# All MLP steps, weight decoding included, put into one planned list of steps

## The chip, the cores and the metric

The kernel runs on one core of one Trainium2 chip. The metric is device time in microseconds (us) of one execution. TensorE is called PE, VectorE DVE, ScalarE ACT, GpSimd POOL, and SyncE, which issues all DMAs here, SP.

## The reference

Inputs are q, k, v of shape 4 x 8 x 576 x 64 and the weights of two further layers. Cut to what matters:

```
attn = softmax(mask(q k^T / 8)) v          # 8 heads, window 32, plain or with dilation 4
x    = attn as (4, 576, 512)
moe  = sum over the best 2 of 4 experts of gate * (causal attention of x with wq, wk, wv) wo[e]
xn   = (moe - mean) / sqrt(var + 1e-6) * g_ln
out  = moe + max(xn @ w_ch1, 0) @ w_ch2    # w_ch1: 512 x 2048, w_ch2: 2048 x 512, both arrive as float64
```

The change touches the last line only: the MLP and its weights. The float64 weights are read as pairs of 32-bit words and are turned into float32 pairs (high part and rest) by the kernel itself.

## The kernel before

The 2304 tokens are 18 tiles of 128 tokens. The moe result of a tile lies in `x2(i)`; it is written by a product called `pwo` (L840) and a copy. For the MLP the tiles form five groups: four of four tiles, 512 tokens each, and the last of two tiles, 256 tokens. The hidden size 2048 is cut in 16 slices f of 128. For each slice there are two weight tiles, x = 0 (from w_ch1) and x = 1 (from w_ch2).

Steps of the MLP:

- `norm_tile` (L992): a tile is centred into `xg` (one buffer, by ACT or DVE), turned by four PE transposes (`pxt`, L1008) and written as `xn`, in two halves, each by ACT (L1017) for the high part and DVE (L1019) for the rest.
- `decode(f, x)` (L884): a DMA of 512 KB into `ws` (two buffers), then a chain of one buffer each: ACT square `d_sq` (L916), DVE L920 and L922 into `d_t`, DVE L926 and L929 into `d_pw`, POOL sum L932, DVE L935, for x = 0 a POOL product with g_ln (L940), ACT cast to the high part of `wp` (L942), POOL rest (L944).
- `mlp_group(fs, gi, ...)` (L1025): for each slice in fs, 12 matmuls of 512 columns into a PSUM bank `phid` (L1043), then ACT relu into `ht` (L1051) and DVE rest (L1053). `ht` has three buffers. Then for each tile of the group, 3 matmuls per slice into a bank `pout` (L1068), and a DVE sum into x2 (L1075). At the last slice pair x2 goes out by DMA.

A job is one call of `mlp_group`. `phid` and `pout` use the three banks of tag "a" in the first jobs, and the two banks "s" and three banks "t" in the later ones.

What sets the order: inside `tc.manual_schedule()` every step is a generator that asks for engine time (`op`), buffers (`acq`) or facts (`key`). `run_chains` (L198) goes through them like a clock: each time it emits the step that can start first by its table of costs, ties by rank. What is emitted so stays in that order on each engine, and each engine runs its queue in order. Before, the list held the attention layers, norms, the decoding of slices 0 to 2, and the jobs (0, 1) and (2) for groups 0 to 2. Everything behind it (slice pair (0, 1) for groups 3 and 4, slice 3, and all later pairs) was written out by the loop at the end (`run`, `jobs`, `weights`): one weight decoding ahead of each job. These steps are outside the manual schedule, and the order on the engines shows that a scheduler of the framework then interleaves them, so they do not stand exactly as written.

Of the kernel before, what the change touches and what calls it, by code (L numbers as in the profile page):

```python
# [8 lines left out]
F32R = mybir.dt.float32r  # L9
# [14 lines left out]
def windowed_attention_moe_mlp(  # L24
# [795 lines left out]
    def out_proj(b, i):  # L820
# [21 lines left out]
        if i == 0:  # L842
            give("yhs", tp)
        elif last(("yh", b), NT - 1):
            give("yh", tp)
        t, e = yield either(("ACT", act(DM)), ("DVE", dve(DM)), deps=[tp])
# [18 lines left out]
    places.update(ht=[], ws=[], dsq=[], dt1=[], dpw=[], xg=[])  # L865

    def open_mlp():
# [10 lines left out]
        for tag, n in (("ht", 1), ("ws", 2), ("dsq", 1), ("dt1", 1), ("dpw", 1), ("xg", 1)):  # L878
            give(tag, t, n)
        put("wts", at=t)  # L880
# [3 lines left out]
    def decode(f, x):  # L884
# [20 lines left out]
        else:  # L905
            if f // GF % 2 == 0:
                w = wts.tile([P, 2, DM], F32R, tag=f"wp{f % GF}{x}", name="wp")
            else:
                w = att.tile([P, 2, DM], F32R, tag=("yh", "yl", "woh", "wol")[2 * (f % GF) + x], name="wp")
# [115 lines left out]
    def mlp_group(fs, gi, htag, otag):  # L1025
# [7 lines left out]
        hs = []  # L1033
        for f in fs:
            t0 = max(t, (yield key("wf", f, 0)))
            w1h, w1l = WF[f, 0]
            tb = yield acq(htag)
# [8 lines left out]
            ta = yield acq("ht")  # L1046
            pool, tag = HT.pop(0)
            ht = pool.tile([P, 2, 4 * P], F32R, tag=tag, name="ht")
            hh, hl = ht[:, 0], ht[:, 1]
# [7 lines left out]
        for x, i in enumerate(grp):  # L1057
# [12 lines left out]
            if x == len(grp) - 1:  # L1070
                for *_, pool, tag in hs:
                    HT.append((pool, tag))
                give("ht", tp, len(hs))
            tx = yield op("DVE", 660.0, [tp, tr])
            nc.vector.scalar_tensor_tensor(x2(i), po, rstd[:, i:i + 1], x2(i), op0=ALU.mult, op1=ALU.add)  # L1075
            give(otag, tx)
            if fs[-1] == NF - 1:
                for bb, s0, p0, m in rows_of(order[i]):
                    nc.sync.dma_start(out[bb, s0:s0 + m, :], x2(i)[p0:p0 + m])
# [5 lines left out]
    with tc.manual_schedule():  # L1085
# [21 lines left out]
        for f in range(3):  # L1107
            for x in range(2):
                chain(41.0 + 2 * f + x, decode(f, x))
# [6 lines left out]
        for gi in range(EARLY):  # L1116
            chain(44.0 + gi, mlp_group((0, 1), gi, "a", "a"))
            chain(48.0 + gi, mlp_group((2,), gi, "a", "a"))
        run_chains()


    def run(gen):
        ask = next(gen)
        while True:
            value = 0.0
            if ask[0] == "op" and len(ask[1]) > 1:
                value = 0.0, ask[1][0][0]
            try:
                ask = gen.send(value)
            except StopIteration:  # L1130
                return


    jobs = [((0, 1), gi) for gi in range(EARLY, len(groups))]
    jobs += [((3,), gi) for gi in range(EARLY)] + [((2, 3), gi) for gi in range(EARLY, len(groups))]
    for f0 in range(2 * GF, NF, GF):
        jobs += [((f0, f0 + 1), gi) for gi in range(len(groups))]

    def weights(fs):
        for f in fs:  # L1140
            for x in range(2):
                run(decode(f, x))
                yield

    fill = weights((3,))
    for x, (fs, gi) in enumerate(jobs):
        if (fs[-1], 0) not in WF:
            for _ in fill:
                pass
        if x == 0 or fs != jobs[x - 1][0]:  # L1150
            if fs != (2, 3):
                for _ in fill:
                    pass
                nf = fs[-1] + 1 if fs[-1] > 1 else 3
                fill = weights(range(nf, min(nf + GF, NF)) if nf > 3 else (3,))
        next(fill, None)
        run(mlp_group(fs, gi, "s", "t"))
# [28 lines left out]
```

## Time and profile before

| | us |
|---|---|
| median of 3 runs | 777.85 (777.27 to 781.38) |
| the profiled execution | 777.57 |
| its span on the core | 775.8 |
| PE busy | 728.6 (94%) |
| DVE busy | 535.2 (69%) |
| ACT busy | 303.4 (39%) |
| POOL busy | 207.0 (27%) |

The span begins at the first instruction of the core and ends with the last. A time such as "at 417.57" is us from the span's start. A row of a timeline gives start, length, engine, line, operation, result and operands, shapes, count, and in brackets idle time just before, with the engine and line that ended it. Neighbouring matmuls overlap in the rows: how fast they follow is read from the starts.

### The profile page before, as it was taken

Reading aid. Unit: us, or ns where it says so; the run is one execution under the profiler, and the core shown is the slowest. Engines: PE = TensorE matmul, PEld = TensorE weight load, DVE = VectorE, ACT = ScalarE, POOL = GpSimd, SP = SyncE. Lnnn points to the kernel's source line nnn. Section 1 sums busy time; section 2 is a strip of 40 time slices with the busy share of each in tenths; the row PEclk is TensorE's granted clock in tenths of the full one; section 3 lists DMA queues with packets and bytes.
Section 4 is the critical chain, followed back from the end, with each engine's and each line's share of the span. In section 5 each row is a group of like instructions: output and inputs, shape, how many; then the busy total and the mean of one; then the engine's idle time right before and its main releaser. Section 6 shows DMA issues by size and latency. Waiting matters only on the chain.

```text
span 775.8 us, 13793 instructions
## 1 busy us (share of the span) xinstructions
PE 728.6 (94%) x5196; PEld 606.8 (78%) x5196; DVE 535.2 (69%) x1357; ACT 303.4 (39%) x817; POOL 207.0 (27%) x245
## 2 busy tenths in 40 slices
PE   6788899998999998998997999999999999999997
PEld 5677778986888686876775888888888888888886
DVE  5647898599867989898657788657466475644333
ACT  4454576466555776574325222212121121211110
POOL 3242154022302234434004445214032140220000
PEclk9869999999999999899998999999999999999999
DMA  8681143033302111011001212102011010000114
GB/s 146 123 159 31 28 102 71 21 67 74 63 17 52 39 61 55 28 52 31 1 1 55 82 54 82 55 27 82 1 55 54 26 57 27 28 1 0 41 69 136
DMA packets 87890, 41.80 MB, mean 54 GB/s; under 512 B 74384, under 2 KB 83088, under 8 KB 87824
## 3 DMA queue, kind: packets, MB, share of 16 engines
q1 hardware_dynamic: 87824, 40.92, 20.9%
q8 instruction: 41, 0.67, 0.4%
q14 instruction: 25, 0.20, 0.1%
HBM read 36.19 MB, written 4.72 MB: 53 GB/s over the span
## 4 chain that ended last, share of the span: by engine, by line
PE 71%; DVE 20%; ACT 5%; DMA 2%; issue 2%; POOL 1%; DVEq 0%; SPq 0%; ACTq 0%; POOLq 0%
PE pout L1068 26%; PE phid L1043 25%; PE pp L624 3%; PE pv L521 2%; PE pwo L840 2%; PE ppt L767 2%; PE s L436 2%; DVE nm L711 1%; PE ptr L380 1%; PE ppt L464 1%; DMA nat<-in_k_dram 1%; DVE xl L497 1%; DVE klz L647 1%; DVE sc L448 1%; DVE mx L446 1%
## 5 line engine op out<-in xcount | busy, mean ns | idle before, releaser
L1043 PE MATMUL phid<-xn,wp 128*128 128x512 f32 (+1 forms) x960 | 218.0, 374 | 2.3 <-ACT xn L1017 1.2
L1068 PE MATMUL pout<-wp,ht 128*128 128x512 f32 x864 | 216.0, 395 | 0.3 <-DVE ht L1053 0.3
L1043 PEld LDWEIGHTS phid<-xn,wp 128*128 128x128 f32 x960 | 169.7, 190 | 37.0 <-ACT xn L1017 1.6
L1068 PEld LDWEIGHTS pout<-wp,ht 128*128 128x128 f32 x864 | 159.8, 188 | 36.3 <-DVE ht L1053 0.7
L1075 DVE SCALAR_TENSOR_TENSOR x2a<-pout,rstd,x2a 128x512 f32<-128x512 f32 x124 | 88.7, 746 | 90.4 <-PE pout L1068 90.3
L1051 ACT ACTIVATE ht<-phid 128x512 fp32r<-128x512 f32 (+1 forms) x80 | 44.4, 555 | 216.5 <-PE pout L1068 138.7
L944 POOL TENSOR_TENSOR wp<-d_pw,wp 128x512 fp32r<-128x512 f32 x34 | 46.1, 1357 | 149.2 <-ACT wp L942 138.3
L1053 DVE SCALAR_TENSOR_TENSOR ht<-phid,ht 128x512 fp32r<-128x512 f32 (+1 forms) x80 | 50.1, 632 | 34.2 <-ACT ht L1051 34.2
L932 POOL TENSOR_TENSOR d_pw<-d_pw,d_t 128x512 f32<-128x512 f32 x34 | 43.9, 1290 | 78.6 <-DVE d_pw L929 70.2
L745 POOL TENSOR_SCALAR Pp<-Pp,rs 128x512 f32<-128x512 f32 (+3 forms) x38 | 45.6, 1207 | 71.0 <-DVE rs L738 37.6
L457 POOL TENSOR_TENSOR sc<-sc,rs 128x288 f32<-128x288 f32 x38 | 25.2, 668 | 86.1 <-DVE rs L455 71.7
L242 ACT COPY pT<-ppt 96x384 f32<-96x384 f32 (+4 forms) x77 | 35.2, 466 | 11.0 <-PE ppt L767 8.8
L380 PE MATMUL ptr<-ident,nat 72*128 72x72 f32 (+1 forms) x196 | 26.4, 260 | 12.9 <-DMA nat<-in_q_dram 9.6
L713 ACT ACTIVATE Pp<-s,nm 128x192 f32<-128x192 f32 (+3 forms) x64 | 30.3, 474 | 18.8 <-DVE nm L711 15.0
L942 ACT CAST wp<-d_pw 128x512 fp32r<-128x512 f32 x34 | 21.1, 620 | 40.4 <-DVE d_pw L935 33.7
L696 PE MATMUL s<-KH,SQ 128*128 128x64 f32 (+4 forms) x96 | 34.1, 362 | 1.1 <-ACT Pp L713 1.1
L436 PE MATMUL s<-kT,qT 64*64 64x96 f32 x576 | 34.4, 259 | 0.2 <-ACT kT L242 0.2
L916 ACT ACTIVATE d_sq<-ws 128x512 f32<-128x512 f32 x34 | 22.8, 672 | 28.4 <-DVE d_pw L935 22.0
L380 PEld LDWEIGHTS ptr<-ident,nat 72*128 72x128 f32 (+1 forms) x196 | 20.6, 155 | 15.4 <-DMA nat<-in_q_dram 5.2
L922 DVE SCALAR_TENSOR_TENSOR d_t<-ws,d_t 128x512 int32<-128x512 int32 x34 | 32.1, 944 | 0.6
L436 PEld LDWEIGHTS s<-kT,qT 64*64 64x64 f32 x576 | 31.7, 146 | 0.5 <-issue 0.5
L464 PE MATMUL ppt<-ident,sc 128*96 128x128 f32 x144 | 26.2, 297 | 6.0 <-DVE xl L497 3.5
(164 smaller groups left out, 1374.7 us busy)
## 6 DMA issues: line engine op xcount, KB each, us to landing
ws<-in_moe_w_ch_dram SPq DMA_DIRECT2D x34, 512.0 KB, 3.4
nat<-in_q_dram SPq DMA_DIRECT2D x14, 288.0 KB, 3.7
nat<-in_k_dram SPq DMA_DIRECT2D x14, 288.0 KB
vt<-in_v_dram SPq DMA_DIRECT2D x16, 192.0 KB, 3.7
out_dram<-x2a SPq DMA_DIRECT2D x12, 256.0 KB, 2.1
vt<-in_v_dram SPq DMA_DIRECT2D x32, 48.0 KB, 1.9
out_dram<-x2b SPq DMA_DIRECT2D x4, 256.0 KB, 2.5
vt<-in_v_dram SPq DMA_DIRECT2D x16, 40.0 KB, 2.1
```

The costliest lines, as they stand in the source:

```text
L242: (nc.scalar.copy if engine == "ACT" else nc.vector.tensor_copy)(dst, src)
L380: nc.tensor.transpose(pt[:, pw * c:pw * (c + 1)], nat[:, hf * ch + c].rearrange("p h d -> p (h d)"), ident[:pw, :pw])
L436: nc.tensor.matmul(ps[z, 96 * tt:96 * (tt + 1)], qT[z, 64 * t_:64 * t_ + 64], kT[z, 64 * t_:64 * t_ + 96], start=False, stop=tt == TU - 1)
L696: nc.tensor.matmul(ps[:m, :z - a], SQ[ee][:, q0:q0 + m], KH[ee][:, a:z], start=True, stop=False)
L745: (nc.vector if e == "DVE" else nc.gpsimd).tensor_scalar(Ps[ee][:m, 64:n], Ps[ee][:m, 64:n], rs[:m, ee:ee + 1], None, op0=ALU.mult)
L932: nc.gpsimd.tensor_tensor(pf, pf, t1.bitcast(F32), op=ALU.add)
L944: nc.gpsimd.tensor_tensor(lo, pf, hi.bitcast(F32), op=ALU.subtract)
L1043: nc.tensor.matmul(ph[:, :n_tok], ws[:, c * P:(c + 1) * P], xs[c], start=n == 0, stop=n == 3 * KC - 1)
L1051: nc.scalar.activation(hh[:, :n_tok], ph[:, :n_tok], AF.Relu)
L1053: nc.vector.scalar_tensor_tensor(hl[:, :n_tok], ph[:, :n_tok], 0.0, hh[:, :n_tok].bitcast(F32), op0=ALU.max, op1=ALU.subtract)
L1068: nc.tensor.matmul(po, a_[:, sl], w_, start=n == 0, stop=n == 3 * len(fs) - 1)
L1075: nc.vector.scalar_tensor_tensor(x2(i), po, rstd[:, i:i + 1], x2(i), op0=ALU.mult, op1=ALU.add)
```

## The change

The list of steps now takes all jobs and all decodings. Jobs are numbered in one order, n = 0, 1, 2, ...; the rank is 44 + n. The decoding of slices from 3 on gets a rank three jobs ahead of the first job that needs it. New bookkeeping: the weight buffers of four slices become places that must be acquired before a decoding goes on past its DMA and are given back when the last group has used them (`spent`, and in `out_proj` for the two that lie where wo lay). A job now acquires its `ht` buffer before its 12 `phid` matmuls, not after them, and a key `hts` makes the jobs take `ht` in their order. The jobs after the first six use banks "s" and "t" as before.

```
@@ out_proj
+        if last("wo", NTT):
+            for f in (2, 3):
+                for x in range(2):
+                    give(("w", f, x), tp)
@@ decode
+            tw = yield acq(("w", f % (2 * GF), x))
@@ mlp_group
-    def mlp_group(fs, gi, htag, otag):
+    def spent(f, x, t):
+        if last(("w", f, x), len(groups)) and f != GF:
+            give(("w", f % (2 * GF), x), t)
+    def mlp_group(n, fs, gi, htag, otag):
...
+        if n:
+            yield key("hts", n - 1)
+        unit = n
         for f in fs:
             t0 = max(t, (yield key("wf", f, 0)))
             w1h, w1l = WF[f, 0]
+            ta = yield acq("ht")
+            pool, tag = HT.pop(0)
+            ht = pool.tile([P, 2, 4 * P], F32R, tag=tag, name="ht")
+            hh, hl = ht[:, 0], ht[:, 1]
+            if f == fs[-1]:
+                put("hts", unit, at=0.0)
             tb = yield acq(htag)
             ph = bank(htag, "phid")
...
-            ta = yield acq("ht")
-            pool, tag = HT.pop(0)
-            ht = pool.tile([P, 2, 4 * P], F32R, tag=tag, name="ht")
-            hh, hl = ht[:, 0], ht[:, 1]
+            spent(f, 0, tp)
...
+                for f in fs:
+                    spent(f, 1, tp)
...
+                yield op("SP", 100.0, [tx])
@@ the list
-        for gi in range(EARLY):
-            chain(44.0 + gi, mlp_group((0, 1), gi, "a", "a"))
-            chain(48.0 + gi, mlp_group((2,), gi, "a", "a"))
+        jobs = [((0, 1), gi) for gi in range(EARLY)] + [((2,), gi) for gi in range(EARLY)]
+        jobs += [((0, 1), gi) for gi in range(EARLY, len(groups))]
+        jobs += [((3,), gi) for gi in range(EARLY)] + [((2, 3), gi) for gi in range(EARLY, len(groups))]
+        for f0 in range(2 * GF, NF, GF):
+            jobs += [((f0, f0 + 1), gi) for gi in range(len(groups))]
+        for n, (fs, gi) in enumerate(jobs):
+            chain(44.0 + n, mlp_group(n, fs, gi, *("aa" if n < 2 * EARLY else "st")))
+        for f in range(NF):
+            need = min(n for n, (fs, gi) in enumerate(jobs) if f in fs)
+            for x in range(2):
+                chain(41.0 + f + 0.5 * x if f < 3 else 44.0 + need - 3.0 + 0.5 * x, decode(f, x))
         run_chains()
-    def run(gen):
...
-        run(mlp_group(fs, gi, "s", "t"))
```

On PE both orders are the same up to the `pout` matmuls of the first jobs, at 333 us of the trace before. The first place below is PE at the end of the attention part, where the last tiles leave `pwo` and are turned by `pxt` (four matmuls each, six tiles left). Before:

```order
L1068 MATMUL pout<-wp,ht 128x512 x3
L840 MATMUL pwo<-woh,yh_5290 128x512
L840 MATMUL pwo<-wol,yh_5290 128x512
L840 MATMUL pwo<-woh,yl_5291 128x512
L840 MATMUL pwo<-woh,yh_5290 128x512
L840 MATMUL pwo<-wol,yh_5290 128x512
L840 MATMUL pwo<-woh,yl_5291 128x512
L1008 MATMUL pxt<-ident,xg 128x128 x16
L1043 MATMUL phid<-xn_6134,wp 128x512 x2
L1008 MATMUL pxt<-ident,xg 128x128 x4
L1043 MATMUL phid<-xn_6136,wp 128x512
```

Now, from the end of the same last `pwo`:

```order
L840 MATMUL pwo<-woh,yl_5292 128x512
L1018 MATMUL pxt<-ident,xg 128x128 x4
L1089 MATMUL pout<-wp,ht 128x512 x3
L1018 MATMUL pxt<-ident,xg 128x128 x4
L1089 MATMUL pout<-wp,ht 128x512 x3
L1018 MATMUL pxt<-ident,xg 128x128 x4
L1089 MATMUL pout<-wp,ht 128x512 x3
L1018 MATMUL pxt<-ident,xg 128x128 x4
L1067 MATMUL phid<-xn_6119,wp 128x512
```

Nine `pout` matmuls moved from before the last `pwo` to between the four turns; `phid` of group 3 still comes behind the fourth.

The second place is DVE where one slice pair ends and the next begins (the same job boundary in both; `d_t1` and `d_pw` belong to a decoding, x2b1 to the last group of the old pair, ht to the first jobs of the new pair). Before:

```order
L1053 SCALAR_TENSOR_TENSOR ht_7805<-phid_7792,ht_7805 128x512
L1075 SCALAR_TENSOR_TENSOR x2b1_6104<-pout_7760,rstd_84,x2b1_6104 128x512
L1075 SCALAR_TENSOR_TENSOR x2b1_6104<-pout_7768,rstd_84,x2b1_6104 128x512
L926 TENSOR_SCALAR d_pw_7943<-d_t1_7940 128x512
L929 SCALAR_TENSOR_TENSOR d_pw_7943<-ws_7935,d_pw_7943 128x512
L1053 SCALAR_TENSOR_TENSOR ht_7821<-phid_7808,ht_7821 128x512
```

Now:

```order
L936 TENSOR_SCALAR d_pw_7395<-d_t1_7383 128x512
L939 SCALAR_TENSOR_TENSOR d_pw_7395<-ws_7158,d_pw_7395 128x512
L1098 SCALAR_TENSOR_TENSOR x2b1_6030<-pout_7397,rstd_84,x2b1_6030 128x512
L945 SCALAR_TENSOR_TENSOR d_pw_7395<-d_sq_7381,d_pw_7395 128x512
L1098 SCALAR_TENSOR_TENSOR x2b1_6030<-pout_7411,rstd_84,x2b1_6030 128x512
L930 TENSOR_SCALAR d_t1_7429<-ws_7342 128x512
L932 SCALAR_TENSOR_TENSOR d_t1_7429<-ws_7342,d_t1_7429 128x512
L1074 SCALAR_TENSOR_TENSOR ht_7363<-phid_7364,ht_7363 128x512
L936 TENSOR_SCALAR d_pw_7450<-d_t1_7429 128x512
L939 SCALAR_TENSOR_TENSOR d_pw_7450<-ws_7342,d_pw_7450 128x512
L1074 SCALAR_TENSOR_TENSOR ht_7436<-phid_7437,ht_7436 128x512
```

The rest of the new pair's first slice (ht_7805 before, ht_7363 now) stood ahead of the old pair's last sums; it now stands behind them and behind six operations of decodings.

## Rows read from the trace of the kernel before

**Rows 1.** Part 1 of the page: busy time, share, instructions.
```profile
PE 728.6 (94%) x5196; PEld 606.8 (78%) x5196; DVE 535.2 (69%) x1357; ACT 303.4 (39%) x817; POOL 207.0 (27%) x245
```
**Rows 2.** Stretches of 10 us: busy PE, PEld, DVE, ACT, POOL, clock, DMA share, GB/s.
```profile
350.00:360.00 10.00, 7.78 (x40) 5.87 (x38) 10.00 (x23) 5.63 (x15) 7.63 (x6) 1.00 0.19 52
...
410.00:420.00 10.00, 4.93 (x20) 3.45 (x21) 8.68 (x20) 5.67 (x14) 5.59 (x5) 0.71 0.16 54
```
**Rows 3.** The same columns, a stretch of 50 us.
```profile
500.00:550.00 50.00, 50.00 (x230) 41.19 (x229) 30.31 (x48) 10.30 (x18) 12.85 (x10) 1.00 0.14 43
```
**Rows 4.** Timeline of PE, its waits between 354 and 366 us.
```profile
355.55 0.63 PE L1008 MATMUL pxt<-ident,xg 128*128 128x128 f32 x4 [1.18 <-DVE xn L1019]
357.22 3.04 PE L1043 MATMUL phid<-xn,wp 128*128 128x512 f32 x12 [1.04 <-DVE ht L1053]
...
364.93 0.63 PE L1008 MATMUL pxt<-ident,xg 128*128 128x128 f32 x4 [0.50 <-DVE xn L1019]
```
**Rows 5.** Timeline of PE from the last pwo on.
```profile
408.96 0.60 PE L1008 MATMUL pxt<-ident,xg 128*128 128x128 f32 x4
411.21 0.65 PE L1008 MATMUL pxt<-ident,xg 128*128 128x128 f32 x4 [1.65 <-ACT xg L1001]
413.82 0.74 PE L1008 MATMUL pxt<-ident,xg 128*128 128x128 f32 x4 [1.96 <-ACT xg L1001]
415.21 1.11 PE L1008 MATMUL pxt<-ident,xg 128*128 128x128 f32 x4 [0.65 <-DVE xg L1003]
417.57 1.22 PE L1043 MATMUL phid<-xn,wp 128*128 128x512 f32 x2 [1.24 <-ACT xn L1017]
418.59 1.05 PE L1008 MATMUL pxt<-ident,xg 128*128 128x128 f32 x4
419.30 5.93 PE L1043 MATMUL phid<-xn,wp 128*128 128x512 f32 x21
```
**Rows 6.** Timelines of ACT and DVE in the same stretch.
```profile
412.78 0.38 ACT L1017 ACTIVATE xn<-pxt 128x256 fp32r<-128x256 f32 x1 [0.49 <-DVE xn L1019]
413.06 0.71 ACT L1001 ACTIVATE xg<-x2b,mva 128x512 f32<-128x512 f32 x1
...
414.67 0.49 DVE L1003 TENSOR_SCALAR xg<-x2b,mva 128x512 f32<-128x512 f32 x1 [0.99 <-PE pxt L1008]
```
**Rows 7.** Groups of instructions from 430 to 750 us: count, busy, mean ns, idle before.
```profile
L944 POOL TENSOR_TENSOR wp<-d_pw,wp 128x512 fp32r<-128x512 f32 x25 | 34.2, 1367 | 110.7 <-ACT wp L942 99.8 <-DVE ht L1053 11.0
L932 POOL TENSOR_TENSOR d_pw<-d_pw,d_t 128x512 f32<-128x512 f32 x24 | 31.0, 1293 | 51.8 <-DVE d_pw L929 50.0 <-PE pout L1068 1.8
L922 DVE SCALAR_TENSOR_TENSOR d_t<-ws,d_t 128x512 int32<-128x512 int32 x24 | 24.2, 1010 | 0.6
...
L929 DVE SCALAR_TENSOR_TENSOR d_pw<-ws,d_pw 128x512 f32<-128x512 uint32 x24 | 16.5, 686 | 0.3
...
L940 POOL TENSOR_TENSOR d_pw<-d_pw,g_in 128x512 f32<-128x512 f32 x12 | 13.9, 1156 | 18.1 <-DVE d_pw L935 18.1
L926 DVE TENSOR_SCALAR d_pw<-d_t 128x512 int32<-128x512 int32 x24 | 10.1, 422 | 10.8 <-POOL wp L944 10.8
```
**Rows 8.** Timeline of all engines from 523 to 530 us.
```profile
523.52 2.96 PE L1043 MATMUL phid<-xn,wp 128*128 128x512 f32 x12
...
526.58 0.60 ACT L1051 ACTIVATE ht<-phid 128x512 fp32r<-128x512 f32 x1 [3.60 <-PE phid L1043]
...
527.21 0.69 DVE L1053 SCALAR_TENSOR_TENSOR ht<-phid,ht 128x512 fp32r<-128x512 f32 x1 [1.25 <-ACT ht L1051]
...
528.58 1.15 POOL L940 TENSOR_TENSOR d_pw<-d_pw,g_in 128x512 f32<-128x512 f32 x1 [1.18 <-DVE d_pw L935]
528.59 0.67 ACT L916 ACTIVATE d_sq<-ws 128x512 f32<-128x512 f32 x1 [1.41 <-DVE d_pw L935]
...
528.88 1.41 DVE L922 SCALAR_TENSOR_TENSOR d_t<-ws,d_t 128x512 int32<-128x512 int32 x1
529.77 0.62 ACT L942 CAST wp<-d_pw 128x512 fp32r<-128x512 f32 x1 [0.51 <-POOL d_pw L940]
```

More of the change, by code (lines that the diff above doesn't have):

```diff
@@ L865, in windowed_attention_moe_mlp @@
     places.update(ht=[], ws=[], dsq=[], dt1=[], dpw=[], xg=[])
+    places.update({("w", f, x): [] for f in range(4) for x in range(2)})
     def open_mlp():
@@ L879, in open_mlp @@
             give(tag, t, n)
+        for f in range(GF):
+            for x in range(2):
+                give(("w", f, x), t)
         put("wts", at=t)
@@ L1106, in windowed_attention_moe_mlp @@
         chain(40.0, open_mlp())
-        for f in range(3):
-            for x in range(2):
-                chain(41.0 + 2 * f + x, decode(f, x))
         chain(41.5, inverse_std(0, 4 * EARLY))
@@ L1115, in windowed_attention_moe_mlp @@
                 chain(41.2 + gi + 0.1 * x, norm_tile(gi, x))
-        for gi in range(EARLY):
-            chain(44.0 + gi, mlp_group((0, 1), gi, "a", "a"))
-            chain(48.0 + gi, mlp_group((2,), gi, "a", "a"))
-        run_chains()
-    def run(gen):
[L1123 to L1156, printed above, removed]
-        run(mlp_group(fs, gi, "s", "t"))
+        jobs = [((0, 1), gi) for gi in range(EARLY)] + [((2,), gi) for gi in range(EARLY)]
[7 more added lines that the diff above has]
+            need = min(n for n, (fs, gi) in enumerate(jobs) if f in fs)
+            for x in range(2):
+                chain(41.0 + f + 0.5 * x if f < 3 else 44.0 + need - 3.0 + 0.5 * x, decode(f, x))
+        run_chains()
 _INS = ['q', 'k', 'v', 'moe_w_gate', 'moe_wq', 'moe_wk', 'moe_wv', 'moe_wo', 'moe2_g_ln', 'moe2_w_ch1', 'moe2_w_ch2']
```

## The prediction

> **What bounds the kernel now.** I read the busy shares first, then the stretches, then PE's own timeline where a stretch is not full, then the groups of the weight decoding. PE is busy 728.6 of 775.8 us [rows 1]. The MLP part from 430 us on is full: the stretch from 500 to 550 us has PE busy 50.00 of 50 with 230 matmuls, that is 0.217 us each, at the full clock level (1.00) [rows 3]. All those matmuls stay, so nothing can be won there; it can only be lost. What can be won lies before 430 us, and only after 333 us, since up to there the order is unchanged. There the trace has two holes:
>
> - 355 to 365 us: waits of 1.18, 1.04 and 0.50 us, together 2.72 [rows 4]. All three are ended by DVE, which is busy 10.00 of 10 us from 350 to 360 [rows 2]. So this hole is DVE's load, not a lack of PE work in the order.
> - 409 to 418 us: waits of 1.65, 1.96, 0.65 and 1.24 us, together 5.50 [rows 5]. Four tiles are turned one behind the other, because `xg` has one buffer: ACT writes it, PE turns it, ACT takes the first half of `xn`, and only then writes the next `xg` [rows 6]. PE is busy 4.93 of 10 us and its granted clock falls to 0.71 in the mean [rows 2], part of the time at the lower of its two levels, 1.2 instead of 2.4 GHz. The 21 matmuls at 419.30 take 5.93 us where 21 x 0.217 = 4.56 would do: 1.37 lost. The two at 417.57 take 1.02 to the next start instead of 0.43, the turn at 418.59 0.71, where I put 0.4 (an estimate, from the length of 0.60 of the one at 408.96 and the overlap that such rows have). The clock costs some 2.3 us.
>
> The most that could be won is thus 2.72 + 5.50 + 2.3 = 10.5 us of the profiled execution's 777.57 (span 775.8, and 1.77 around it). The median of the runs is 777.85, 0.28 more; I make the sum against 777.57. A measurement of this kernel can tell about 0.5% (3.9 us) from no change.
>
> **The turns at 409 us.** Nine `pout` matmuls, 9 x 0.217 = 1.95 us, move from ahead of the last `pwo` to between the turns. PE was dense ahead of it, so the turns begin 1.95 us earlier, at 407.0, and the 1.95 us of work lies in the waits. If the chain of turns took as long as before, all of 1.95 would be won. It takes a little longer: before, the fourth `xg` was written by DVE in 0.49 us (414.67) as soon as the third turn had ended, now all six are ACT's. An ACT-made tile takes 413.82 - 411.21 = 2.61 us from turn to turn, against 1.39 for the fourth; and DVE now has a decoding and two more pout sums between its parts of `xn`, which ACT's second half waits for (the 0.49 at 412.78 is this wait [rows 6]). I place the turns at 407.0, 409.2, 411.8 and 414.4 and `phid` of group 3 a further 415.21 to 417.57 = 2.36 us later less the DVE share, at 416.1: 1.5 us won. Bounds: nothing, if the longer chain eats all of it; 5.50 + 2.3 = 7.8 if work were found for every wait and the clock stayed up. I take 1.5, because the next work for PE is closed: slice 3 of groups 0 to 2 ranks behind the jobs of groups 3 and 4, and the `hts` key keeps it from overtaking. For the clock I take nothing: of the nine us PE works 1.95 + 4 x 0.4 = 3.6, and it fell before from a similar share.
>
> **The attention part, 333 to 407 us.** The same steps in another mix. DVE has the same operations there, and a full engine in one order is full in another. `ht` before `phid` lets fewer `phid` run ahead, which spreads them thinner. I take 0; bounds: 2.72 won, 3 lost (another hole of the size of [rows 4]).
>
> **The end and the DMAs.** The last job now has its own 12 half-width `phid` directly ahead of its own 12 `pout`, where before 6 `pout` of the job ahead stood between. The second slice's rest comes 0.25 (PE's result) + 0.38 + 0.43 us (half-size relu and rest, about 0.6 of the 0.60 and 0.69 of [rows 8]) behind the last `phid`, and PE needs it after 0.65 + 0.43: I take 0.2 lost; bounds 0 and 0.6. SP issues the same 34 loads of weights and the same output tiles, all loads ahead of all outputs; a load is issued when its stage is free and has one whole decoding, over 6 us, to land. Nothing for that. A decoding now waits for its weight place ahead of all its steps but the DMA, where before only the cast had to: for slice 3 that place is free behind the last `pwo`, and it is needed two jobs after the turns (24 + 24 and 24 half-width + 12 matmuls, some 15 us), against two decodings of 6 to 7 us. It is just in time, and the later slices have half a period of the pairs.
>
> **The long MLP part.** This is the term that decides. Before, PE has the whole next job's 24 `phid` done before it needs them. Now `ht` comes first, with three buffers: two belong to the running job, so only one slice's 12 `phid` can be ahead. The second slice's stand between the jobs, with 6 to 9 of the job after as cover (1.3 to 1.95 us), plus 3 `pout` of the first slice (0.65). The way PE - relu - rest takes 0.25 + 0.60 + 0.69 with 0.1 of handing over, some 1.6 us [rows 8]: covered, if ACT and DVE are free.
>
> They are not free in half of the time. The four decodings of a slice pair run back to back. One is serial by its single buffers: from `d_pw` on 0.42 + 0.69 + 1.29 + 0.69 + 1.16 + 0.62 + 1.37 = 6.2 us with the product by g_ln [rows 7, 8]. I place one such boundary in the new order. Take 0 where PE begins the pouts of group 3 of the old pair. The first decoding's DVE operations, with the three sums and one rest between them, bring POOL's sum to 3.7, DVE's next to 5.9, the g_ln product to 7.1, the cast to 7.8, POOL's rest to 9.2. The second follows: `d_pw` 10.4, POOL 11.8, DVE 12.6, then the square on ACT (0.67) to 13.2. PE meanwhile, at 0.217 per matmul: 24 pouts to 5.2, 15 half-width `phid` to 6.9, then 12 `phid` of the new first slice among 12 `pout` of the last group to 12.1, 12 of the second slice to 14.7. The first slice's relu finds ACT in the square and ends at 13.8; its rest stands on DVE behind L922, which starts at 13.5 beside POOL's product and ends about 14.4, so the rest ends at 15.1. PE wants that bank back at 14.7 for group 1, since "s" has two banks, and gets it at 15.2: 0.5 us. After that the second slice is in time (17.6 against 18.4), and so are the third and fourth decodings, by 0.1 to 0.5 us.
>
> There are six such bursts (slices 4 to 15 in pairs): 6 x 0.5 = 3.0 us lost. Bounds: 0 if a burst starts half a us sooner; and if both L922 ahead of the point take 1.41 as at 528.88 instead of 0.69 [rows 8], 1.44 later less the 0.3 I counted, 1.6 per burst, 9.8 in all. I take 0.5, since the mean of L922 is 1.01 [rows 7], which is about what I put.
>
> What L922 costs beside POOL is shown by 1.41 against a POOL product of 1.15 that began 0.30 earlier [rows 8]. The Trainium skill's page "SBUF — State Buffer", section "Who interferes with whom", says that a VectorE instruction with two SBUF inputs and a GpSimd one that reads SBUF exclude each other: the later blocks until the first ends. The trace agrees, roughly: 1.41 is 0.85 of waiting and 0.69 of work, less overlap. By that rule the L922 at 13.5 waits to 13.75 and ends at 14.45, as I have it; but one that starts with the product would take 1.85, and 6 x 0.4 more would make 2.4 us.
>
> **Sum.** 777.57 - 1.5 + 0 + 0.2 + 3.0 = 779.3 us.
>
> **Rivals.**
> - Faster: the list finds work for the holes, and the long part stays dense. For it: the nine pouts do stand in the hole, and the 0.5 us is a difference of two placed times, so it may be nothing. Against it: [rows 2, 4] show DVE as the bound in the first hole, and in the second only 1.95 us of work is at hand. If the second hole and its clock go and the rest is unchanged: 777.57 - 7.8 = 769.8.
> - Slower: ACT and DVE order. One mechanism, in each boundary of slice pairs: relu and rest stand behind square, cast and L922 of a decoding, and PE waits for the bank or `ht`. For it: only one slice's look-ahead is left. Against it: my placing gives a third of that. At 1.6 us per burst: 777.57 - 1.5 + 0.2 + 9.8 = 786.1. It decides from (3.9 + 1.3) / 6 = 0.9 us per burst on.
> - The change does nothing that is seen: the long part is full by [rows 3] in any order, and the waits of [rows 4, 5] belong to DVE and ACT chains that it does not shorten: 777.6. This is within the same band as my forecast.
>
> **How the numbers follow.** Forecast and no effect together 0.41 (own range 775 to 781.7), faster rival 0.30, slower rival 0.29. The range to hold 8 of 10 reaches into both rivals: from 769.5 to 786. Chances: faster by over 0.5% 0.30, within 0.41, slower 0.29.
>
> **What would show it.** In the new trace, from 430 us on: PE busy 50 of 50 in every stretch says that the third term is 0; waits of `phid` on DVE's `ht` rest, some six times and 47 us apart (204 matmuls of 0.217 and 24 of half that in a pair's five jobs), say that it is right, and their mean is its size. At the turns: four waits of `pxt` and `phid` that sum to about 4, with `phid` of group 3 near 416. A clock of 1.00 from 410 to 420 would show that I gave the filled hole too little. I am wrong in kind if the waits in the long part are for weights (`wp` from POOL) or for the `pout` banks.

## The result, and the profile after

The changed kernel takes 770.09 us (median of 4 runs, 769.31 to 772.0) where the kernel before takes 777.89 (777.27 to 781.38): a ratio of 0.9894, with 0.9859 to 0.9929 as its interval. It is faster; the forecast was 779.3, no change. The span of the profiled execution goes from 775.8 to 768.9 us.

Where the 6.9 us went can be read by three marks on PE. The first is the `pxt` directly ahead of the first `pout` (333.06 before, 332.59 after): up to there PE's order is the same. The second is the last `pwo` (408.73 and 403.32), the third the end.

| Stretch | before | after | difference |
|---|---|---|---|
| start to first mark | 333.06 | 332.59 | -0.47 |
| first mark to last `pwo` | 75.67 | 70.73 | -4.94 |
| last `pwo` to the end | 367.07 | 365.58 | -1.49 |

Nine `pout` moved from the second stretch into the third. At 0.233 us each (read below) that is 2.10 us. For equal work the attention part thus won 2.84 us and what lies behind the last `pwo` won 3.59. From the first mark to the end it is 442.74 and 436.31, 6.43 less; this figure is used below as "from the mark", since an unchanged repeat of the kernel after gave 436.31 again while its first mark came 1.6 us sooner.

**The stretches**, kernel after, columns as in [rows 2]:

```profile
350.00:360.00 10.00, 10.00 (x63) 7.56 (x61) 9.29 (x26) 6.65 (x18) 2.33 (x2) 1.00 0.00 0
...
410.00:420.00 10.00, 7.88 (x37) 5.67 (x37) 7.30 (x15) 6.18 (x14) 4.41 (x4) 1.00 0.31 94
```
```profile
500.00:550.00 50.00, 50.00 (x229) 41.13 (x228) 30.53 (x49) 10.02 (x18) 12.94 (x10) 1.00 0.14 43
```

The first hole is gone (PE 10.00 where [rows 2] have 7.78); POOL has 2 instructions there and not 6. In 410 to 420 the clock is 1.00 where it was 0.71. The stretch from 500 to 550 is as full as in [rows 3], and so is every one of 50 us from 450 to 750.

**The turns**, PE from the last `pwo` on, kernel after, against [rows 5]:

```profile
403.32 0.39 PE L840 MATMUL pwo<-woh,yl 128*128 128x512 f32 x1
403.55 0.60 PE L1018 MATMUL pxt<-ident,xg 128*128 128x128 f32 x4
403.90 0.94 PE L1089 MATMUL pout<-wp,ht 128*128 128x512 f32 x3
405.29 0.66 PE L1018 MATMUL pxt<-ident,xg 128*128 128x128 f32 x4 [0.45 <-ACT xg L1011]
406.61 0.97 PE L1089 MATMUL pout<-wp,ht 128*128 128x512 f32 x3 [0.67 <-DVE x2a L1098]
408.30 0.66 PE L1018 MATMUL pxt<-ident,xg 128*128 128x128 f32 x4 [0.71 <-ACT xg L1011]
408.71 0.94 PE L1089 MATMUL pout<-wp,ht 128*128 128x512 f32 x3
410.92 0.66 PE L1018 MATMUL pxt<-ident,xg 128*128 128x128 f32 x4 [1.27 <-ACT xg L1011]
412.05 1.88 PE L1067 MATMUL phid<-xn,wp 128*128 128x512 f32 x6 [0.47 <-ACT xn L1027]
...
417.12 4.12 PE L1067 MATMUL phid<-xn,wp 128*128 128x512 f32 x21
...
422.82 4.35 PE L1089 MATMUL pout<-wp,ht 128*128 128x512 f32 x18
427.01 2.99 PE L1067 MATMUL phid<-xn,wp 128*128 128x256 f32 x18
```

From the first turn to `phid` of group 3 it is 8.50 us, hardly less than 8.61 in [rows 5]; but PE waits 3.57 us of it instead of 5.50.

The row of 21 `phid` must not be set against the 21 of [rows 5], since a timeline merges widths. Kernel after, 417.4 to 421.2 us by width:

```profile
L1067 PE MATMUL phid<-xn,wp 128*128 128x512 f32 x12 | 3.0, 402 | 0.0
L1067 PE MATMUL phid<-xn,wp 128*128 128x256 f32 x9 | 1.2, 282 | 0.0
```

What the clock cost before is read from starts. At a clock of 1.00 the 18 `pout` at 422.82 take 4.19 us to the next start, 0.233 each. The 21 `phid` of [rows 5], all 512 wide, would have taken 4.89 us so; to the next start of before, a turn, they took 5.77:

```profile
425.07 0.60 PE L1008 MATMUL pxt<-ident,xg 128*128 128x128 f32 x4
```

That is 0.9 lost. The two `phid` ahead of them and the turn between took 1.73, where 0.82 would do (a turn takes 0.35 from 403.55 on): 0.9 again. So the clock cost some 1.8 us behind the start of this `phid`, and the kernel after has none of it.

**The end**, the last sums on DVE, kernel before, then after:

```profile
770.87 1.41 DVE L1075 SCALAR_TENSOR_TENSOR x2b<-pout,rstd,x2b 128x512 f32<-128x512 f32 x2 [1.76 <-PE pout L1068]
```
```profile
763.66 0.75 DVE L1098 SCALAR_TENSOR_TENSOR x2b<-pout,rstd,x2b 128x512 f32<-128x512 f32 x1 [0.60 <-PE pout L1089]
765.05 0.75 DVE L1098 SCALAR_TENSOR_TENSOR x2b<-pout,rstd,x2b 128x512 f32<-128x512 f32 x1 [0.64 <-PE pout L1089]
```

The last `pout` matmul starts at 770.67 and 764.61.

**The decoding**, groups from 430 to 750 us, kernel after, against [rows 7]:

```profile
L932 DVE SCALAR_TENSOR_TENSOR d_t<-ws,d_t 128x512 int32<-128x512 int32 x22 | 15.2, 690 | 0.5
L930 DVE TENSOR_SCALAR d_t<-ws 128x512 int32<-128x512 int32 x22 | 13.2, 598 | 0.0
```

L932 is L922 of before: 690 ns where it took 1010.

**What had been overlooked.** Over the whole span the kernel before has this instruction 34 times, the kernel after 32:

```profile
L922 DVE SCALAR_TENSOR_TENSOR d_t<-ws,d_t 128x512 int32<-128x512 int32 x34 | 32.1, 944 | 0.6
```
```profile
L932 DVE SCALAR_TENSOR_TENSOR d_t<-ws,d_t 128x512 int32<-128x512 int32 x32 | 22.4, 701 | 0.7
```

The loop behind the list asked for `weights((3,))` twice, so slice 3 was decoded twice. As the first copy stood behind the list, the planner (`run_chains`) did not know of it; its first steps lie in the attention part all the same, put between the planned ones. Its two L922 lie at the first hole of [rows 4]:

```profile
350.69 0.80 DVE L922 SCALAR_TENSOR_TENSOR d_t<-ws,d_t 128x512 int32<-128x512 int32 x1
...
358.22 0.67 DVE L922 SCALAR_TENSOR_TENSOR d_t<-ws,d_t 128x512 int32<-128x512 int32 x1
```

The kernel after has none between 344 and 372 us; there slice 3 waits for its weight place ahead of its first step.

One thing that these steps did can be read at the first wait. The POOL sum of the first decoding of slice 3 runs beside L740, a product of the attention part on DVE. `run_chains` keeps marked steps such as these two apart, if it knows of both. Kernel before:

```profile
353.28 1.26 DVE L740 TENSOR_TENSOR Ph<-Pp,rs 128x128 f32<-128x128 f32 x1
```
```profile
353.10 1.29 POOL L932 TENSOR_TENSOR d_pw<-d_pw,d_t 128x512 f32<-128x512 f32 x1 [2.16 <-DVE rs L738]
```

The same product in kernel b_list (below), where this decoding is planned:

```profile
352.67 0.28 DVE L740 TENSOR_TENSOR Ph<-Pp,rs 128x128 f32<-128x128 f32 x1
```

L740 ends at 354.54, 0.15 us behind the POOL sum. So 0.98 of the 10.00 us for which DVE is called busy is a wait for POOL, and the rest of `xn` for which PE waits 1.18 us stands behind it. This is read from the rows; no run took this one product apart.

### The profile page after: what moved, and what is told of

Its sections match the earlier page's. It is cut to its first block, busy times and chain, and to the rows that moved or that the text cites. A ratio compares the mean times of both kernels' runs of the same rounds, so it can differ in the third digit from the quotient of the medians.

```text
span 768.9 us, 13753 instructions
## 1 busy us (share of the span) xinstructions
PE 728.3 (95%) x5196; PEld 606.1 (79%) x5196; DVE 531.2 (69%) x1343; ACT 302.1 (39%) x818; POOL 197.8 (26%) x239
## 4 chain that ended last, share of the span: by engine, by line
PE 68%; DVE 21%; ACT 5%; DMA 3%; issue 2%; POOL 1%; SPq 0%; DVEq 0%; ACTq 0%; POOLq 0%
PE phid L1067 25%; PE pout L1089 25%; PE pp L624 3%; PE ppt L767 2%; DVE nm L711 2%; PE pwo L840 2%; PE ptr L380 2%; PE pv L521 1%; DMA nat<-in_k_dram 1%; PE s L436 1%; PE ppt L464 1%; DVE xl L497 1%; DVE klz L647 1%; DVE sc L448 1%; DMA nat<-in_q_dram 1%
## 5 line engine op out<-in xcount | busy, mean ns | idle before, releaser
L1089 PE MATMUL pout<-wp,ht 128*128 128x512 f32 x864 | 218.5, 395 | 0.9 <-DVE x2a L1098 0.7
L1098 DVE SCALAR_TENSOR_TENSOR x2a<-pout,rstd,x2a 128x512 f32<-128x512 f32 x124 | 92.3, 748 | 52.9 <-PE pout L1089 51.7
L942 POOL TENSOR_TENSOR d_pw<-d_pw,d_t 128x512 f32<-128x512 f32 x32 | 41.3, 1291 | 169.5 <-DVE d_pw L939 165.1
L745 POOL TENSOR_SCALAR Pp<-Pp,rs 128x512 f32<-128x512 f32 (+3 forms) x37 | 44.0, 1194 | 68.1 <-DVE rs L738 56.2
L954 POOL TENSOR_TENSOR wp<-d_pw,wp 128x512 fp32r<-128x512 f32 x32 | 44.2, 1383 | 39.0 <-ACT wp L952 36.7
L436 PE MATMUL s<-kT,qT 64*64 64x96 f32 x576 | 35.1, 263 | 0.2 <-ACT kT L242 0.2
L767 PE MATMUL ppt<-ident,Pp 128*128 128x128 f32 x160 | 29.6, 285 | 2.6 <-ACT V L242 0.8
```

Of the source, the lines that this page charges most:

```text
L436: nc.tensor.matmul(ps[z, 96 * tt:96 * (tt + 1)], qT[z, 64 * t_:64 * t_ + 64], kT[z, 64 * t_:64 * t_ + 96], start=False, stop=tt == TU - 1)
L745: (nc.vector if e == "DVE" else nc.gpsimd).tensor_scalar(Ps[ee][:m, 64:n], Ps[ee][:m, 64:n], rs[:m, ee:ee + 1], None, op0=ALU.mult)
L767: nc.tensor.transpose(pt[:, P * (j - 1):P * j], Ps[ee][:, k0:k0 + P], ident)
L942: nc.gpsimd.tensor_tensor(pf, pf, t1.bitcast(F32), op=ALU.add)
L954: nc.gpsimd.tensor_tensor(lo, pf, hi.bitcast(F32), op=ALU.subtract)
L1089: nc.tensor.matmul(po, a_[:, sl], w_, start=n == 0, stop=n == 3 * len(fs) - 1)
```

## The experiments

Time and ratio to before are from runs interleaved with the kernel before on the same chip, the interval in brackets. There were five such sets, in which the kernel before took 777.15 to 778.42 us, so kernels of different sets are compared by the ratio. Names with b are edits of the kernel before, names with a of the kernel after. The last columns are from each profile: PE's waits at 340 to 372 us, the `pout` between the last `pwo` and `phid` of group 3 that stand between turns, PE's waits in that stretch, the lowest clock of a 10-us stretch from 400 to 430, and the time from the mark to the end.

| Kernel | us | ratio | 1st hole | pout | waits | clock | from the mark |
|---|---|---|---|---|---|---|---|
| before | 777.89 | | 2.72 | 0 | 5.50 | 0.71 | 442.74 |
| b_once | 776.62 | 0.9987 [0.9963, 1.0011] | 2.70 | 0 | 5.51 | 0.59 | 443.39 |
| b_late | 774.74 | 0.9957 [0.9935, 0.9979] | 0.51 | 0 | 5.82 | 0.67 | 440.74 |
| b_ht | 775.75 | 0.9966 [0.9947, 0.9984] | 1.58 | 3 | 5.74 | 0.67 | 441.42 |
| b_list | 768.78 | 0.9874 [0.9846, 0.9902] | 0 | 12 | 1.75 | 0.87 | 434.39 |
| after | 770.09 | 0.9894 [0.9859, 0.9929] | 0.19 | 9 | 3.57 | 1.00 | 436.31 |
| a_again | 773.07 | 0.9931 [0.9902, 0.9960] | 0.19 | 9 | 3.57 | 1.00 | 436.31 |
| a_early3 | 768.08 | 0.9874 [0.9841, 0.9906] | 0 | 9 | 4.08 | 1.00 | 434.83 |
| a_htlate | 773.84 | 0.9957 [0.9938, 0.9975] | 0.18 | 3 | 5.22 | 0.61 | 440.63 |
| a_both | 773.09 | 0.9940 [0.9917, 0.9962] | 0 | 3 | 5.13 | 0.66 | 438.61 |
| a_nofill | 778.21 | 1.0001 [0.9983, 1.0020] | 0.19 | 0 | 8.96 | 0.58 | 442.36 |
| a_nofill2 | 778.72 | 1.0010 [0.9988, 1.0032] | 0.21 | 0 | 8.96 | 0.50 | 443.21 |
| a_xg2late | 769.62 | 0.9894 [0.9865, 0.9922] | 0.19 | 9 | 2.59 | 1.00 | 434.39 |
| a_best | 768.02 | 0.9867 [0.9843, 0.9891] | 0 | 9 | 1.69 | 0.89 | 433.59 |

### The first hole: slice 3's steps, and ht ahead of phid

**b_once**: before, slice 3 decoded once.
```
-        if x == 0 or fs != jobs[x - 1][0]:
+        if x and fs != jobs[x - 1][0]:
```


> The kernel before, with the weights of slice 3 decoded once. The loop at its end writes that decoding twice: the page of before has 34 weight loads and 34 of L922, of after 32. This run drops the second copy; the first copy's DVE steps still stand in the attention part (L922 at 350.69 and 358.22 in before). Theory A (the first hole of 2.72 us at 355 to 365 is the price of these early steps on a full DVE): the hole stays, waits there 2 to 3 us, time 777 to 778. Rival B (the hole goes because ht is acquired ahead of phid): the same. Rival C (the second copy, standing behind the last pwo, is what cost time): 775 or less, with the waits after 409 us smaller.


Measured: no difference. The second copy itself cost nothing that can be told; the one that is left still lies in the attention part, and the hole is there.

**b_late**: as b_once, with slice 3 in the list and, but for its load, held until the last `pwo`.
```
...
+        if f == 3:
+            tw = yield key("wofree")
```


> The kernel before, slice 3 decoded once and all its steps but the load held until the last pwo (in the list, by a key); all else as before. Theory A: the waits of PE between 354 and 366 us fall from 2.72 to under 0.7, the last pwo comes 2 to 3 us earlier, time 775 to 776. Rival B: the hole stays at 2 to 3 us, time 777.5 or more. Rival C: like the run with one copy.


The first hole nearly goes (0.51), the second stays.

**b_ht**: before, with `ht` acquired ahead of `phid` in the six early jobs.
```
...
+                ta = yield acq("ht")
...
+                ht = pool.tile([P, 2, 4 * P], F32R, tag=tag, name="ht")
...
```


> The kernel before, with ht acquired ahead of phid, in job order, in the six early jobs alone; slice 3 still decoded twice and early. Rival B: the waits between 350 and 370 us fall to under 0.7, time 775 to 776. Theory A: waits of 2 us or more stay there, time 777 to 779.


Part of the first hole goes, the second stays.

**a_early3**: after, with slice 3 waiting for its place only at its cast, so that its steps lie in the attention part again.
```
+            if f != 3:
+                tw = yield acq(("w", f % (2 * GF), x))
...
+        if f == 3:
+            tw = yield acq(("w", 3, x))
```


> The changed kernel, with slice 3 let off waiting for its weight place until its cast: its DVE, ACT and POOL steps come in the attention part again (rows 906 and 941 of DVE's order, ahead of the last statistics at 984; 977 and 996 without the edit). Theory A: waits of 1.5 to 3 us come back between 345 and 370 us, time 771.5 to 773 against 770.1. Rival B: no such waits, 770.1 within 0.5.


The theory that these steps make the hole fell: DVE has them again and PE has no wait there.

**a_htlate**: after, with `ht` acquired behind `phid`, as before. **a_both**: this and a_early3 together.


> The kernel after, with ht taken behind the phid of a slice again, as before, in all jobs: more phid may run ahead of their relu. Theory A (ht first is part of what fills the first hole, since phid is spaced out by it, even with slice 3's decoding out of the attention part): waits of 1 us or more come back at 350 to 370 and the time is 1 to 3 us longer than the kernel after, 771 to 773. Theory B (without slice 3's early steps the DVE is not full there and the place of ht does not matter): waits at 350 to 370 stay under 0.6 us in sum, and the time is within 1 us of 770. For the long part both theories expect 50.00 of 50; if ht first had been a loss there, as the prediction had it, this kernel would be 1 to 3 us faster than the kernel after.

> The kernel after, with both of the things undone that were each undone alone before: slice 3 waits for its weight place only at its cast, so that its other steps come in the attention part again, and ht is taken behind the phid of a slice. Theory A (the first hole of the kernel before needs both, the early steps on DVE and phid running ahead of relu): waits of 1 to 3 us in sum come back between 345 and 370, and the time is above that of the kernel with ht late alone, 773.8, by 1 to 3 us: 775 to 777. Theory B (it is a third thing, the tiles of groups 3 and 4 being in the list, or the way the planner mixes the steps, that keeps the hole away): no wait above 0.6 us there, and the time stays at 772 to 774.5.


The first hole stays away in both, so the theory that it takes both fell too. What they lose, they lose behind the last `pwo`, where only 3 `pout` are left between the turns and the clock falls to 0.61 and 0.66. Against a_early3, a_both has six `pout` fewer there (1.40 us of work) and takes 3.8 us more from the mark; the place of `ht` differs too.

**b_list**: before, with slice 3 decoded once and in the list, as early as it comes, only its cast held.
```
-        for f in range(3):
+        for f in range(4):
-    fill = weights((3,))
+    fill = iter(())
...
+        if f == 3:
+            tw = yield key("wofree")
         t = yield op("ACT", 610.0, [t, tw])
```


> The kernel before, with slice 3 decoded once and in the list, its steps planned as early as they come and only its cast held until the last pwo (as the kernel after with early steps has it); phid stays ahead of ht. Theory A (the first hole was made by steps that the planner knew nothing of, put between its own): waits at 345 to 370 fall from 2.72 to under 0.6 us though DVE has the same steps there, and the time is 2 to 5 us below before: 772.5 to 775.5. Theory B (DVE is simply too full there with these steps and phid ahead): the waits stay at 1.5 us or more and the time is at 775.5 to 777.5.


This settles the first hole. The same steps lie at the same place, no wait is left, and PE's stretch is full (9.88 of 10 us) beside a DVE that is nearly as full as before. Kernel b_list:

```profile
351.07 0.68 DVE L924 SCALAR_TENSOR_TENSOR d_t<-ws,d_t 128x512 int32<-128x512 int32 x1
358.85 0.68 DVE L924 SCALAR_TENSOR_TENSOR d_t<-ws,d_t 128x512 int32<-128x512 int32 x1
```
```profile
350.00:360.00 10.00, 9.88 (x51) 7.82 (x49) 9.71 (x26) 6.46 (x15) 4.97 (x5) 1.00 0.18 53
410.00:420.00 10.00, 10.00 (x48) 8.04 (x47) 8.57 (x17) 5.71 (x12) 4.08 (x4) 0.96 0.32 104
```

And b_once, where the same steps are not planned:

```profile
350.00:360.00 10.00, 7.80 (x35) 5.78 (x34) 9.93 (x24) 5.47 (x12) 6.70 (x5) 1.00 0.17 52
410.00:420.00 10.00, 6.41 (x20) 4.70 (x21) 8.32 (x17) 4.03 (x10) 5.17 (x4) 0.59 0.23 69
```

The planner that knows of the steps puts other work around them, and in doing so keeps twelve `pout` for the turns. This one slice in the list gives as much as the whole change: 434.39 from the mark, 1.9 us less than the kernel after.

### The turns: work between them, and the clock

**a_nofill**: after, with the tiles of groups 3 and 4 not normalised until the `pout` of the sixth job are issued. **a_nofill2**: only the first turn held; PE's order at the turns is the same, nine `pout` and then five turns. The edit of a_nofill2:
```
...
+        if gi == EARLY and x == 0:
+            yield key("job", 2 * EARLY - 1)
         tb = yield acq("a")
```


> The kernel after, with one key more: the tiles of groups 3 and 4 are not normalised before the pouts of the sixth early job are issued, so that these nine pouts stand in one piece ahead of the four turns again, as in the kernel before, and nothing lies between the turns. Theory A (the pouts between the turns are what shortens the second hole and keeps the clock at 1.00): PE's waits between the last pwo and phid of group 3 grow from 4.3 to about 5.5 us or more, the granted clock falls to about 0.7 in one stretch of 10 us between 400 and 430, and the time is 1.95 us (nine pouts at 0.217) plus about 2 us of clock longer than the kernel after: 772 to 774. Theory B (the clock stays because the first hole is gone, and the order at the turns is worth little): the clock stays at 1.00 and the time is within 1.5 us of the kernel after, 769 to 771.5.

> The kernel after, with the first turn alone held until the nine pouts of the sixth early job are issued; its statistics and its xg may be made before. This takes out what the other kernel without the pouts between the turns also did, namely to hold the making of xg. PE's order is the same as there: nine pouts in one piece, then five turns. Theory A (with work between the turns gone, the wait and the clock are what costs): waits between the last pwo and phid of group 3 of 6 to 9 us, clock below 0.8 in 410 to 420, time 775 to 778. Theory B (what cost in the other kernel was that xg was made late): waits near 5.5 us, clock as in the kernel before or better, time 772 to 774.


Both lose nearly all that the change won: 6.1 and 6.9 us from the mark, 8 by the medians, where 2 to 4 were expected of the first. The second shows that it is not a late xg. Kernel a_nofill2:

```profile
402.65 2.27 PE L1091 MATMUL pout<-wp,ht 128*128 128x512 f32 x9
405.41 0.63 PE L1020 MATMUL pxt<-ident,xg 128*128 128x128 f32 x4 [0.49 <-DVE rstd L964]
408.12 1.11 PE L1020 MATMUL pxt<-ident,xg 128*128 128x128 f32 x4 [2.08 <-ACT xg L1011]
411.19 1.11 PE L1020 MATMUL pxt<-ident,xg 128*128 128x128 f32 x4 [1.96 <-ACT xg L1011]
414.78 1.12 PE L1020 MATMUL pxt<-ident,xg 128*128 128x128 f32 x4 [2.48 <-ACT xg L1011]
417.85 1.12 PE L1020 MATMUL pxt<-ident,xg 128*128 128x128 f32 x4 [1.95 <-ACT xg L1011]
```
```profile
410.00:420.00 10.00, 4.38 (x15) 3.35 (x16) 5.19 (x13) 5.25 (x12) 3.71 (x3) 0.50 0.28 87
420.00:430.00 10.00, 10.00 (x49) 8.38 (x48) 5.30 (x11) 4.17 (x9) 1.30 (x1) 0.92 0.04 14
```

Four turns at the lower level (1.11 us instead of 0.66), and a clock of 0.50. A fifth turn stands ahead of `phid` here, 3.07 us behind the fourth, so these kernels pay more than the missing cover alone; the two shares were not separated.

**a_xg2late**: after, with a second `xg` buffer from the last `pwo` on. **a_best**: this and a_early3.
```
-        xg = wts.tile([P, DM], F32, tag="xg", name="xg", bufs=1)
+        xg = wts.tile([P, DM], F32, tag="xg", name="xg", bufs=2)
```


> The kernel after, with a second buffer for xg that the planner gets only at the last pwo, so that the order ahead of it is unchanged: ACT can write the next xg while PE turns the one before. Theory A (what is left of the second hole, 4.3 us, is the chain xg, turn, half of xn, next xg through one buffer): the waits of pxt and phid behind the last pwo sum to under 2.5 us, phid of group 3 starts 1.5 to 4 us sooner behind the last pwo than in the kernel after (8.7 us there), and the time is 1.5 to 4 us below it: 766 to 768.6. Theory B (the next stage of the chain, xn's halves on ACT and DVE and the sums of groups 3 and 4 that the tiles are made from, is as late): the waits move to phid, their sum stays at 4 to 4.5 us and the time within 1 us of 770.

> The kernel after, with slice 3's steps early (768.08 alone) and the second xg buffer from the last pwo on (769.62 alone). Theory A (the two act at different places, so they add): phid of group 3 starts within 8.5 us of the last pwo with 30 matmuls in one piece behind it, and the time is 766 to 768, a ratio to before of 0.983 to 0.987. Theory B (both only fill the same hole, the one at the turns): the time is that of the better alone, 768 to 769.


From the mark the buffer gives 1.9 us, the early steps 1.5 and both together 2.7: more than either alone, less than the sum. The median of a_xg2late does not tell its 1.9 from nothing. a_best has the lowest median that was measured, at the border of its two theories, and is 0.8 us from the mark below b_list.

### The long part: what slack is left

**a_noshare4**: after, decodings from slice 4 on planned without the rule that keeps DVE's and POOL's marked steps apart.
```
+        dv, pl = ("DVE*", "POOL*") if f < 4 else ("DVE", "POOL")
```


> The kernel after, with the decodings from slice 4 on planned without the planner's rule that DVE's and POOL's marked steps do not lie beside each other; the instructions are the same. Theory A (this rule keeps the DVE decoding steps at 0.69 us and so keeps the long part full): L933 (d_n, the second DVE product of a decoding) goes from 0.69 back to about 1.0 us in the mean, and PE shows waits of phid or pout in the long part, up to 0.5 us in each of six bursts, 770 to 773. Theory B (the steps are longer but the long part has slack enough): the mean rises to 0.9 us or more, PE stays at 50.00 of 50 in every stretch from 450 to 750, and the time stays within 1 us of 770. Theory C (the rule hardly matters, the order alone keeps the steps apart): the mean stays under 0.8 us and the time is the same.


771.56 us, 0.9919 [0.9889, 0.9949], 436.26 from the mark: no difference. The step's mean rises from 690 to 881 ns, less than expected, and PE stays dense.

**a_dose1** and **a_dose**: after, with this step (L933) done twice and three times; **b_dose**: before, with it done three times. Nothing that sets the order knows of it.
```
+        for _ in range(3 if f >= 4 else 1):
             nc.vector.scalar_tensor_tensor(t1, nh, -0x40000000, t1, ...)
```


> The kernel after, with d_n done twice instead of once from slice 4 on: 0.69 us more on DVE in every decoding. Theory A (the slack at a boundary of slice pairs is above 0.69 us per decoding, or 1.4 for two in a row): PE dense from 450 to 750, 769 to 772. Theory B (the edge is below that): PE waits for ht or phid's bank in the bursts, half of the 34 us or less, 774 to 790.

> The kernel after, with the second DVE product of a decoding done three times instead of once from slice 4 on (it gives the same bits again), and the planner not told of it: 2 x 0.69 = 1.4 us more on DVE in every decoding, at the place where the prediction saw relu and rest fall behind. Theory A (the long part has several us of slack at each boundary of slice pairs, so the 0.5 us that were predicted were nowhere near): PE stays at 50.00 of 50 in the stretches from 450 to 750 and the time is within 1.5 us of 770. Theory B (the long part is at its edge, and only the measured length of the steps keeps it there): PE waits for phid or pout in each of six bursts, 0.5 to 1.5 us each, and the time is 3 to 9 us longer, 773 to 779.

> The kernel before, with d_n done three times instead of once from slice 4 on, not told to anything that sets the order: the same dose that cost the kernel after 34 us. Theory A (the order of before has the whole next job's phid done ahead and so more slack, as the prediction had it): 777 to 790, clearly less than 34 us more. Theory B (the slack is the same in both, since it is DVE's place in the decoding and not phid's look-ahead that decides): 805 to 815.


Measured: a_dose1 783.99 us (1.0077 [1.0050, 1.0104]), a_dose 804.09 (1.0342 [1.0310, 1.0373]), b_dose 782.28 (1.0043 [1.0022, 1.0063]). From the mark a_dose1 loses 14.6 us and a_dose 35.1. By the length of 0.69 the dose is 16.6 and 33.1 us in 24 decodings; the busy time of this step, in which waits beside POOL are contained, grew by 27.4 and 45.0. Half and more of what DVE took thus reaches the end. In b_dose it grew by 46.2, and the order of before loses 3.3. PE's waits from 430 us on, kernel a_dose:

```profile
PE pout L1090 <- DVE ht L1075: 13.9, 9, 2.1
PE phid L1068 <- DVE ht L1075: 7.8, 5, 2.3
```

Kernel b_dose:

```profile
PE pout L1069 <- DVE x2a L1076: 1.7, 2, 1.1
PE pout L1069 <- ACT ht L1052: 0.3, 1, 0.3
```

One of the waits of a_dose, all engines:

```profile
531.91 0.60 ACT L1073 ACTIVATE ht<-phid 128x512 fp32r<-128x512 f32 x1 [0.97 <-PE phid L1068]
532.00 3.12 DVE L933 SCALAR_TENSOR_TENSOR d_t<-ws,d_t 128x512 int32<-128x512 int32 x3
...
535.04 0.68 DVE L1075 SCALAR_TENSOR_TENSOR ht<-phid,ht 128x512 fp32r<-128x512 f32 x1
...
535.77 2.34 PE L1068 MATMUL phid<-xn,wp 128*128 128x512 f32 x9 [1.11 <-DVE ht L1075]
```

relu is done at 532.51, its rest stands behind the product until 535.04, and PE waits for the bank: the mechanism of the prediction's third term, with 3.12 us in place of a step of 0.69 to 1.41. PE's waits are 21.7 us of the 35.1; the clock, at 0.96 to 0.98 in four of the stretches of 50 us, accounts for part of the rest, which was not followed further.

**a_again**: the kernel after once more, beside b_list.


> The kernel after, unchanged, as the standard for this set: 769.5 to 771.5, a ratio to before of 0.987 to 0.993. If it is at 0.9867 or below, the version with early steps and a second xg buffer (768.02, 0.9867) is no faster than it.


Its median of 8 runs is 773.07, 3 us above the first set's and outside what was expected; its runs go from 768.56 to 775.59. By this set the change is worth 0.7%, by the first 1.1%, and the intervals overlap. From the mark its profile (span 767.3) has 436.31, as that of the kernel after. The runs' spread is thus larger than the differences among the faster kernels; for these the time from the mark, of one profile each, is what there is.

## Why the prediction was wrong

- **What bounds**: read rightly. Most of the gain comes from the two holes, and the long part is full in both. Of the 10.5 us named as the most that could be won, 6.4 came, 0.9 of it behind the last matmul, where nothing was looked for.
- **The length of a matmul, misread.** The 0.217 us are 50 us through 230 matmuls, but some 24 of these are half as wide. One of 512 columns takes 0.233. Nine `pout` are thus 2.10 us and not 1.95, the clock of the second hole cost some 1.8 us and not 2.3, and a slice pair takes 204 x 0.233 + 24 x 0.117 = 50.3 us and not 47.
- **The long part, 3.0 lost: 0.** This was the term that decides, and the step that failed is its 0.5 us per burst, the difference of two placed times. With 0.233 in place of 0.217 the same placing has PE at 5.6, 7.3, 12.9 and 15.7; the bank is back at 15.2, before PE wants it at 15.7, so by this placing no wait was due. L922's contention was carried over from [rows 7] besides: in the new order this step is 0.69, not 1.01. Without the planner's rule it is 0.88, and still nothing waits; so rule and order each do part of it. The mechanism is real and its direction right: a dose on DVE makes just these waits, 14.6 us for one more step per decoding, while the old order takes two more for 3.3 us.
- **The attention part, taken as 0: 2.84 won.** The failed step is "DVE has the same operations there, and a full engine in one order is full in another". The operations are not the same (two decodings fewer between 344 and 372 us), since the count of "the same 34 loads" was not made: it is 34 and 32. And the second half fails by itself: b_list has the same steps with DVE 9.71 of 10 us busy and no wait. DVE at 10.00 beside waits showed an order that did not know of part of DVE's work, not too much work.
- **The turns, 1.5 won: 2.21 at the start of `phid` of group 3.** The chain was placed well: 2.10 us earlier by the nine `pout`, and 8.50 us to `phid` where 9.1 were put. The step that failed is "For the clock I take nothing": the clock stayed at 1.00, which spared some 1.8 us behind that start. At the last matmul 0.5 of it is left (353.1 and 352.6 us from there to it), since two waits of together 0.73 us now lie behind the start, and the rest was not followed. With the nine `pout` in a piece (a_nofill2) the clock falls to 0.50 and the change's gain is lost, though the first hole stays closed.
- **The end, 0.2 lost: 0.4 won.** The last sum on DVE ends 1.61 us behind the start of the last `pout` matmul in the kernel before and in all kernels made from it, and 1.19 in the kernel after and all made from that. Before, the last two sums stand back to back; now each starts as its `pout` is done. From the last sum to the end it is 3.56 and 3.11 us; these 0.45 are not put down to the change, since b_once, with the old order, has 3.14.
- **Rivals**: the faster one gave 769.8 and was within 0.3 us, by luck: it had all of the second hole and its clock (7.8) and nothing of the first, where 3.59 and 2.84 came. The range held the time.

What stays open: why b_late keeps no `pout` for the turns and b_list twelve is the planner's arithmetic, which was not followed; nor was how much of a_nofill's loss is the clock and how much its fifth turn.

## What to carry to other kernels

Count the instructions of each kind in both kernels before saying that the work is the same: work that stands behind a planned list is put between the planned steps by something else, and a full engine with waits around it may be that and not a lack of time. A stretch with little work for PE costs twice, in waits and then in clock for what follows, so a few matmuls between its waits can be worth more than their length: here six of them, 1.40 us of work, went with 3.8 us. And a part that is dense in the trace is not a part with slack: a dose of extra work shows how near its edge it is: here one more step per decoding cost 14.6 us after the change, and two more 3.3 us before it. And take the length of an instruction from rows of one shape: a mean over two widths was 7% off, and the term that decided the forecast hung on less.

## What the runs showed of the hardware

The wait of the decodings for POOL, which lengthened L922 in the kernel before [rows 8], did not end. It moved to L930, a DVE instruction with one input, whose mean went from 466 ns in the kernel before to 600 over the whole span. DVE and POOL, kernel after:

```profile
451.51 1.01 DVE L930 TENSOR_SCALAR d_t<-ws 128x512 int32<-128x512 int32 x1
459.95 0.62 DVE L930 TENSOR_SCALAR d_t<-ws 128x512 int32<-128x512 int32 x1
```
```profile
450.94 1.30 POOL L954 TENSOR_TENSOR wp<-d_pw,wp 128x512 fp32r<-128x512 f32 x1 [1.99 <-ACT wp L952]
...
459.00 1.29 POOL L954 TENSOR_TENSOR wp<-d_pw,wp 128x512 fp32r<-128x512 f32 x1 [0.73 <-ACT wp L952]
```

POOL's instructions end at 452.24 and 460.29, L930 ends 0.28 us after each; its shortest is 0.415. Of the 32 L930 of this kernel 15 start while a two-input instruction of POOL runs, and every one of them ends 0.28 us after it. The Trainium skill's page "SBUF — State Buffer", section "Who interferes with whom", says that `tensor_scalar` too can enter a mode that takes the ports which VectorE and GpSimd share, and that the one issued first keeps them for its whole instruction. The trace agrees.

The first mark, up to which the order is the same, came between 329.87 and 336.56 us in these profiles, and at 332.59 and 330.99 for the same kernel. A cause was not looked for.
